# Reading the moving operand of the feed-forward products in turn from the two halves of its row

## The chip, the cores and the metric

The kernel runs on one core of one Trainium2 chip. The metric is the time of one execution on the device, in microseconds. Before the change it is 862.88 us, the median of three runs (862.77 to 863.19).

## The reference

A retention layer (attention without softmax, with a decay that falls with the distance of the positions) is followed by two feed-forward layers. The batch is 4, with 8 heads, 576 positions and a head dimension of 64, so that 2304 tokens of width 512 reach the feed-forward layers. Everything is float32.

```
scores = (q @ k.T) / sqrt(64)                # for each batch and head
ret    = scores * D                          # D[i,j] = gamma_h**(i-j) for j <= i, else 0
x      = ret @ v                             # -> 2304 x 512
x      = lrelu(x @ moe_w_in) @ moe_w_out     # 512 -> 2048 -> 512, slope 0.01
y      = elu(x @ moe2_w_in) @ moe2_w_out     # 512 -> 2048 -> 512, alpha 1
```

## The kernel before, in words

The tokens stand in five blocks (`SIZES`): four of 512 (128 positions of each of the four batch entries) and a small one of 256. The 2048 hidden features are cut into 16 groups of 128, and those into four quarters of four groups (`NQ`, `FQ`). A unit of work is (layer `m`, quarter `q`, block, group); the units run in that order, so that for each quarter all five blocks are passed.

Each float32 product is made from three products in the float32r type. Every operand is split into a rounded part and a rest (`wh`, `wl` for weights, `xh`, `xl` for the input, `gh`, `gl` for the activated hidden values), and high times high, low times high and high times low are summed in one bank of PSUM.

`moe_h` makes the hidden values of a unit: 12 products (L399), with a 128 x 128 piece of the input weights as the stationary operand and 512 tokens as the moving operand. The result is 128 features by 512 tokens. ScalarE and VectorE apply the nonlinearity and split the result into `gh` and `gl`. `moe_y`, three units later (`LAG`), makes the second product of a unit, 12 products again (L538). In the first layer the output weights are stationary and the 512 tokens of `gh` or `gl` move, so that the result is features by tokens, which is what the next layer reads. In the second layer a 128 x 128 piece of `gh` or `gl` is stationary and the 512 columns of the output weights `wh` or `wl` move, so that the result is tokens by features, as the output is stored. `evac` adds each quarter's result to a sum in SBUF; at the last quarter the first layer's sum is split into the next layer's `xh` and `xl`, and the second layer's is stored.

The block of 256 tokens goes through `moe_h_small` and `moe_y_small`. There the high and the low part lie side by side in one tile of 512 columns, so that one product covers both (L426, L478), and a second product of 256 columns (L431, L478) adds the low part of the weights. In the second layer L478 moves 512 columns of the output weights, as L538 does; the last tile of the kernel is made in two cuts of 256 columns.

In all cases the moving operand is read as one run of 4-byte columns that follow each other in SBUF, and the result is written as one run in PSUM.

The program writes the order of the work out by hand. The retention steps (20 of them) are set between the first units; their products are small float32 ones (L204, L239, L250, L262, L297). Before them TensorE runs 18 products of 512 bfloat16 columns on idle data (L628) in two groups of nine, each with the same stationary operand. The weights come in by the SP queue in pieces of 512 KB and are unpacked and split by ScalarE and VectorE (`split_a`, `split_b`, `split_c`). In `split_a` ScalarE reads every second 4-byte word of the loaded tile (L345, L347):

```
two = raws.pop(key).rearrange("p (n t) -> p n t", t=2)
low, high = two[:, :, 0], two[:, :, 1]
```

Of the kernel before, what the change touches and what calls it, by code (L numbers as in the profile page):

```python
# [17 lines left out]
NT, DM, DFF = B * S, H * D, 2048  # L18
# [11 lines left out]
BOUNDS = [sum(SIZES[:i]) for i in range(len(SIZES) + 1)]  # L30
# [15 lines left out]
def _turned(x):  # L46

    x = x.copy()
    x[:, ::2] = np.roll(x[:, ::2], HC, axis=0)
    return x  # L50


def _decays():
# [30 lines left out]
def retention_moe(  # L84
# [15 lines left out]
    nc = tc.nc  # L100
# [12 lines left out]
    def bank(tag, bufs):  # L113
        return psum.tile([P, 512], F32, tag=tag, bufs=bufs, name=f"ps_{tag}")
# [58 lines left out]
    xx = xpool.tile([P, KC, 2 * SMALL], F32R, tag="xx", name="xx")  # L173
# [206 lines left out]
    gs = {}  # L380
    yb = {}

    def moe_h(u):
        m, q, blk, fs = u
        n = SIZES[blk]
        if blk == NMAIN:
            return moe_h_small(u)
        h = bank("h", 4)
        for i, f in enumerate(fs):
            wh, wl = weights["i", (m * NQ + q) * FQ + f]  # L390
            ops = []
            for kk in range(KC):
                w = slice(kk * P, (kk + 1) * P)
                ops += [(wh[:, w], xh[blk][:, kk, :]), (wl[:, w], xh[blk][:, kk, :])]
            for kk in range(KC):
                w = slice(kk * P, (kk + 1) * P)
                ops += [(wh[:, w], xl[blk][:, kk, :])]
            for k, (a, x) in enumerate(ops):
                nc.tensor.matmul(  # L399
                    h[:, i * n : (i + 1) * n], a, x, start=k == 0, stop=k == len(ops) - 1  # L400
                )
        g = gpool.tile([P, NMAX], F32, tag="g", name="g")
        gh = gpool.tile([P, NMAX], F32R, tag="gh", name="gh", bufs=LAG + 1)
        gl = gpool.tile([P, NMAX], F32R, tag="gl", name="gl", bufs=LAG + 1)
        if m == 0:
            nc.scalar.activation(gh, h, AF.Prelu, alpha=0.01)  # L406
            nc.scalar.activation(g, h, AF.Prelu, alpha=0.01)  # L407
        else:
            nc.scalar.activation(g, h, AF.Relu, scale=-1.0)  # L409
            nc.scalar.activation(g, g, AF.Exp, scale=-1.0)  # L410
            nc.vector.scalar_tensor_tensor(g, g, -1.0, h, ALU.add, ALU.max)  # L411
            nc.vector.tensor_copy(gh, g)
        nc.vector.tensor_tensor(gl, g, gh.bitcast(F32), ALU.subtract)  # L413
        gs[u] = gh, gl

    def moe_h_small(u):

        m, q, blk, fs = u
        n = SMALL
        hs = gpool.tile([P, NMAX], F32, tag="g", name="hs")  # L420
        for i, f in enumerate(fs):
            wh, wl = weights["i", (m * NQ + q) * FQ + f]
            h = bank("h", 4)
            for kk in range(KC):
                w = slice(kk * P, (kk + 1) * P)
                nc.tensor.matmul(  # L426
                    h, wh[:, w], xx[:, kk, :], start=kk == 0, stop=False, skip_group_check=True
                )
            for kk in range(KC):
                w = slice(kk * P, (kk + 1) * P)  # L430
                nc.tensor.matmul(  # L431
                    h[:, :n], wl[:, w], xh[blk][:, kk, :],
                    start=False, stop=kk == KC - 1, skip_group_check=True,
                )
            t = hs[:, i * n : (i + 1) * n]
            nc.scalar.activation(t, h[:, n:], AF.Copy)
            nc.vector.tensor_tensor(t, t, h[:, :n], ALU.add)
        if m == 0:
            g = hs
            nc.scalar.activation(g, hs, AF.Prelu, alpha=0.01)  # L440
        else:
            g = gpool.tile([P, NMAX], F32, tag="g", name="g")
            nc.scalar.activation(g, hs, AF.Relu, scale=-1.0)
            nc.scalar.activation(g, g, AF.Exp, scale=-1.0)
            nc.vector.scalar_tensor_tensor(g, g, -1.0, hs, ALU.add, ALU.max)
        both = []
        for i, tag in enumerate(("gh", "gl")):
            t = gpool.tile([P, NMAX], F32R, tag=tag, name=tag, bufs=LAG + 1)
            part = g[:, i * n : (i + 1) * n]
            nc.scalar.activation(t[:, :n], part, AF.Copy)  # L450
            nc.vector.tensor_tensor(t[:, n:], part, t.bitcast(F32)[:, :n], ALU.subtract)
            both.append(t)
        gs[u] = both

    def moe_y_small(u):
        m, q, blk, fs = u
        n = SMALL
        both = gs.pop(u)
        parts = KC if m == 0 else n // P
        if fs[0] == 0:  # L460
            yb[blk] = [bank("y", 4) for _ in range(parts)]
        y = yb[blk]

        last = m == 1 and q == NQ - 1 and fs[-1] == FQ - 1
        for e in range(parts):
            cuts = [slice(0, DM // 2), slice(DM // 2, DM)] if last and e == parts - 1 else [slice(0, DM)]
            for cut in cuts:
                for t, f in zip(both, fs):
                    wh, wl = weights["o", (m * NQ + q) * FQ + f]
                    if m == 0:  # L470
                        w = slice(e * P, (e + 1) * P)
                        ops = (y[e], wh[:, w], t), (y[e][:, :n], wl[:, w], t[:, :n])
                    else:
                        a, b = t[:, e * P : (e + 1) * P], t[:, n + e * P : n + (e + 1) * P]
                        o = y[e][:, cut]
                        ops = (o, a, wh[:, cut]), (o, a, wl[:, cut]), (o, b, wh[:, cut])
                    for k, (o, a, x) in enumerate(ops):
                        nc.tensor.matmul(  # L478
                            o, a, x, start=f == 0 and k == 0,
                            stop=f == FQ - 1 and k == len(ops) - 1, skip_group_check=True,  # L480
                        )
        if fs[-1] == FQ - 1:
            evac_small(m, q, blk, yb.pop(blk))
# [33 lines left out]
    def moe_y(u):  # L517

        m, q, blk, fs = u
        if blk == NMAIN:  # L520
            return moe_y_small(u)
        gh, gl = gs.pop(u)
        n = SIZES[blk]
        parts, cols = (KC, n) if m == 0 else (n // P, DM)
        if fs[0] == 0:
            yb[blk] = [bank("y", 4)[:, :cols] for _ in range(parts)]
        y = yb[blk]
        for e in range(parts):
            for i, f in enumerate(fs):
                wh, wl = weights["o", (m * NQ + q) * FQ + f]  # L530
                if m == 0:
                    w, g = slice(e * P, (e + 1) * P), slice(i * n, (i + 1) * n)
                    ops = (wh[:, w], gh[:, g]), (wh[:, w], gl[:, g]), (wl[:, w], gh[:, g])
                else:
                    g = slice(i * n + e * P, i * n + (e + 1) * P)
                    ops = (gh[:, g], wh), (gh[:, g], wl), (gl[:, g], wh)
                for k, (a, x) in enumerate(ops):
                    nc.tensor.matmul(  # L538
                        y[e], a, x, start=f == 0 and k == 0, stop=f == FQ - 1 and k == 2
                    )  # L540
        if fs[-1] == FQ - 1:
            evac(m, q, blk, cols, yb.pop(blk))

    def evac(m, q, blk, cols, y):
        if q == 0:
            yp[blk] = big.tile([P, 4, 512], F32, tag="big", name="yp")
        a = yp[blk]
        for e in range(len(y)):
            t = a[:, e, :cols]
            if q == 0:  # L550
                nc.scalar.activation(t, y[e], AF.Copy)
            else:
                nc.vector.tensor_tensor(t, t, y[e], ALU.add)  # L553
            if q == NQ - 1 and m == 0:
                nc.scalar.activation(xh[blk][:, e, :cols], t, AF.Copy)
                nc.gpsimd.tensor_tensor(
                    xl[blk][:, e, :cols], t, xh[blk].bitcast(F32)[:, e, :cols], ALU.subtract
                )
            if q == NQ - 1 and m == 1:
                t0 = BOUNDS[blk] + e * P  # L560
                nc.sync.dma_start(out=out[t0 : t0 + P, :], in_=t)
# [35 lines left out]
    with tc.manual_schedule():  # L597
        qk, v, k = slice(0, 2), slice(2, 3), slice(3, 4)
# [69 lines left out]
        for n in range(len(units) + LAG):  # L668
            u = units[n] if n < len(units) else None
            p = units[n - LAG] if n >= LAG else None  # L670
            s = nxt if nxt < nsteps else None
# [10 lines left out]
            if u:  # L682
                moe_h(u)
# [25 lines left out]
            if p:  # L709
                moe_y(p)  # L710
# [61 lines left out]
```

## Time and profile before

| | |
|---|---|
| median of three runs | 862.88 us (862.77 to 863.19) |
| span of the profiled execution | 862.2 us; it stands 0.7 us under the median |
| TensorE (PE), matmuls | 850.8 us busy, 99% of the span |
| VectorE (DVE) | 502.5 us, 58% |
| ScalarE (ACT) | 347.8 us, 40% |
| GpSimd (POOL) | 85.4 us, 10% |
| mean granted TensorE clock | 0.999 of full speed |

The profile shows one execution. The times of the three runs stand without a profile of their own, so the profiled execution is known by its span, from the first to the last instruction. Matmuls overlap in the records, since each one's recorded length reaches past the start of the next; the rate of TensorE is read from the distance between starts, not from the recorded lengths.

### The profile page before, as it was taken

How to read it: one execution, taken by the hardware profiler on the slowest of the kernel's cores; microseconds unless marked ns; L12 is line 12 of the kernel's file. 1: busy time of each engine (PE TensorE's matmuls, PEld its weight loads, DVE VectorE, ACT ScalarE, POOL GpSimd, SP SyncE). 2: the span in 40 equal slices, each digit the busy share in tenths (PEclk: the TensorE clock that was granted, in tenths of full speed). 3: DMA queues.
4: the chain of work that ended last, by engine and by line, in shares of the span. 5: the costliest groups of instructions: out<-in, count | busy, mean ns of one | idle time of the engine just before them, and what ended most of it. 6: DMA issues, size and time to landing. Idle time of an engine off the chain costs nothing.

```text
span 862.2 us, 11733 instructions
## 1 busy us (share of the span) xinstructions
PE 850.8 (99%) x4664; PEld 702.8 (82%) x4664; DVE 502.5 (58%) x889; ACT 347.8 (40%) x631; POOL 85.4 (10%) x88
## 2 busy tenths in 40 slices
PE   8899999999999999999999999999999999999998
PEld 5778887888888888888888888888888888888886
DVE  5998952465254652556345873657656784675443
ACT  3455444543233432345344643554234442532222
POOL 2564421000000000002222100000000000000000
PEclk9999999999999999999999999999999999999999
DMA  9984420121000220112000220102101220001112
GB/s 335 329 303 145 157 79 9 49 98 50 1 29 21 74 74 1 49 49 69 30 25 25 74 74 0 50 31 68 49 10 40 74 74 0 25 1 49 49 50 74
DMA packets 23143, 60.15 MB, mean 70 GB/s; under 512 B 2864, under 2 KB 6192, under 8 KB 23088
## 3 DMA queue, kind: packets, MB, share of 16 engines
q1 hardware_dynamic: 22800, 59.26, 20.2%
q8 instruction: 37, 0.61, 0.3%
q10 hardware_dynamic: 288, 0.14, 0.1%
q14 instruction: 18, 0.15, 0.1%
HBM read 54.66 MB, written 4.72 MB: 69 GB/s over the span
## 4 chain that ended last, share of the span: by engine, by line
PE 95%; DVE 2%; DMA 1%; ACT 0%; POOL 0%; issue 0%; SPq 0%; DVEq 0%; POOLq 0%
PE ps_y L538 41%; PE ps_h L399 40%; PE ps_y L478 5%; PE ps_h L426 3%; PE ps_h L431 2%; PE ps_h L204 1%; PE ps_h L250 1%; DMA ain<-in_att 1%; DVE ain L222 0%; PE ps_h L297 0%; PE ps_h L262 0%; PE ps_h L239 0%; DVE pf L226 0%; PE ps_y L204 0%; DVE u L362 0%
## 5 line engine op out<-in xcount | busy, mean ns | idle before, releaser
L399 PE MATMUL ps_h<-xh,wil 128*128 128x512 f32 x512 | 199.6, 390 | 1.9 <-POOL wil L375 1.9
L399 PE MATMUL ps_h<-xh,wih 128*128 128x512 f32 x512 | 199.9, 390 | 0.9 <-ACT wih L373 0.6
L413 DVE TENSOR_TENSOR gl<-g,gh 128x512 fp32r<-128x512 f32 x128 | 91.0, 711 | 174.1 <-ACT g L407 168.5
L399 PE MATMUL ps_h<-xl,wih 128*128 128x512 f32 x512 | 136.9, 389 | 0.0
L406 ACT ACTIVATE gh<-ps_h 128x512 fp32r<-128x512 f32 x64 | 38.2, 597 | 196.5 <-PE ps_h L399 196.4
L411 DVE SCALAR_TENSOR_TENSOR g<-g,ps_h 128x512 f32<-128x512 f32 x64 | 44.0, 687 | 122.1 <-ACT g L410 121.9
L399 PEld LDWEIGHTS ps_h<-xh,wil 128*128 128x128 f32 x512 | 96.1, 188 | 22.2 <-POOL wil L375 2.5
L399 PEld LDWEIGHTS ps_h<-xh,wih 128*128 128x128 f32 x512 | 96.1, 188 | 21.5 <-ACT wih L373 1.0
L399 PEld LDWEIGHTS ps_h<-xl,wih 128*128 128x128 f32 x512 | 96.1, 188 | 20.2
L409 ACT ACTIVATE g<-ps_h 128x512 f32<-128x512 f32 x64 | 38.2, 597 | 180.0 <-PE ps_h L399 180.0
L538 PE MATMUL ps_y<-gh,woh 128*128 128x512 f32 x256 | 101.3, 396 | 0.0
L538 PE MATMUL ps_y<-gh,wol 128*128 128x512 f32 x256 | 100.1, 391 | 0.7 <-POOL wol L375 0.7
L538 PE MATMUL ps_y<-gl,woh 128*128 128x512 f32 x256 | 99.8, 390 | 0.0
L538 PE MATMUL ps_y<-woh,gl 128*128 128x512 f32 x256 | 99.7, 390 | 0.0
L538 PE MATMUL ps_y<-wol,gh 128*128 128x512 f32 x256 | 99.7, 390 | 0.0
L538 PE MATMUL ps_y<-woh,gh 128*128 128x512 f32 x256 | 99.6, 389 | 0.0
L553 DVE TENSOR_TENSOR yp<-yp,ps_y 128x512 f32<-128x512 f32 x96 | 59.4, 680 | 0.0
L538 PEld LDWEIGHTS ps_y<-gh,wol 128*128 128x128 f32 x256 | 48.0, 188 | 11.5 <-POOL wol L375 1.1
L538 PEld LDWEIGHTS ps_y<-gh,woh 128*128 128x128 f32 x256 | 48.0, 188 | 10.7 <-ACT woh L373 0.2
L538 PEld LDWEIGHTS ps_y<-woh,gl 128*128 128x128 f32 x256 | 48.1, 188 | 10.1
L538 PEld LDWEIGHTS ps_y<-wol,gh 128*128 128x128 f32 x256 | 48.0, 188 | 9.8
L538 PEld LDWEIGHTS ps_y<-woh,gh 128*128 128x128 f32 x256 | 48.0, 188 | 9.7
(106 smaller groups left out, 1104.6 us busy)
## 6 DMA issues: line engine op xcount, KB each, us to landing
raw<-in_moe_in SPq DMA_DIRECT2D x32, 512.0 KB, 3.3
raw<-in_moe_out SPq DMA_DIRECT2D x32, 512.0 KB, 3.3
ain<-in_att SPq DMA_DIRECT2D x16, 512.0 KB, 6.8
ain<-in_att SPq DMA_DIRECT2D x20, 256.0 KB, 7.3
out<-yp SPq DMA_DIRECT2D x17, 256.0 KB, 2.2
kn<-in_att SPq DMA_DIRECT2D x12, 256.0 KB, 6.2
st<-in_near_v SPq DMA_DIRECT2D x32, 64.0 KB, 5.4
ain<-in_tail_qk SPq DMA_DIRECT2D x4, 256.0 KB, 3.2
```

What stands on the lines that cost most here:

```text
L204: nc.tensor.matmul(sc[j][keys[j], pr * n : (pr + 1) * n], t[r, 1, pr * n : (pr + 1) * n], t[r, 0, pr * n : (pr + 1) * n], start=True, stop ...
L250: nc.tensor.matmul(x[half[j], pr * n : (pr + 1) * n], st[b][:, j, pr, :], t[:, 2 * j, pr * n : (pr + 1) * n], start=pr == 0, stop=n < CH, ...
L399: nc.tensor.matmul(h[:, i * n : (i + 1) * n], a, x, start=k == 0, stop=k == len(ops) - 1)
L406: nc.scalar.activation(gh, h, AF.Prelu, alpha=0.01)
L409: nc.scalar.activation(g, h, AF.Relu, scale=-1.0)
L411: nc.vector.scalar_tensor_tensor(g, g, -1.0, h, ALU.add, ALU.max)
L413: nc.vector.tensor_tensor(gl, g, gh.bitcast(F32), ALU.subtract)
L426: nc.tensor.matmul(h, wh[:, w], xx[:, kk, :], start=kk == 0, stop=False, skip_group_check=True)
L431: nc.tensor.matmul(h[:, :n], wl[:, w], xh[blk][:, kk, :], start=False, stop=kk == KC - 1, skip_group_check=True,)
L478: nc.tensor.matmul(o, a, x, start=f == 0 and k == 0, stop=f == FQ - 1 and k == len(ops) - 1, skip_group_check=True,)
L538: nc.tensor.matmul(y[e], a, x, start=f == 0 and k == 0, stop=f == FQ - 1 and k == 2)
L553: nc.vector.tensor_tensor(t, t, y[e], ALU.add)
```

## The change

A new helper `product` issues every product of both feed-forward layers. It hands TensorE the moving operand in another order: column 0, then the first column of the second half, then column 1, then the second column of the second half, and so on. For 512 columns the two halves are 256 columns, 1024 bytes, apart. Where a tile holds a high and a low part side by side (`parts` is 2), each part has its own two halves, and for an operand of 256 columns the halves are 128 columns, 512 bytes, apart. The result is still written as one run in PSUM, so that each such product leaves its columns in a shuffled order: the tokens of a block are shuffled once more by each of the first three products, and the host puts them right at the end (`_in_order`). In the last product the weights move, and the host shuffles the columns of `moe2_w_out` beforehand so that the features come out in order. The number of instructions, the data that each reads, the stationary operands, the retention part and the transfers' sizes are unchanged.

```diff
+def _in_order(y):
+    for _ in range(3):
+        y = y.reshape(-1, 2, DM).transpose(1, 0, 2).reshape(-1, DM)
+    return y
...
+    def product(out, w, x, parts=1, cut=None, **flags):
+        if parts == 1:
+            x = x.rearrange("p (a n) -> p n a", a=2)
+            if cut:
+                x = x[:, cut.start // 2 : cut.stop // 2, :]
+            out = out.rearrange("p (n a) -> p n a", a=2)
+        else:
+            x = x.rearrange("p (s a n) -> p s n a", s=parts, a=2)
+            out = out.rearrange("p (s n a) -> p s n a", s=parts, a=2)
+        nc.tensor.matmul(out, w, x, **flags)
...
     def moe_h(u):
...
-                nc.tensor.matmul(
-                    h[:, i * n : (i + 1) * n], a, x, start=k == 0, stop=k == len(ops) - 1
-                )
+                product(h[:, i * n : (i + 1) * n], a, x, start=k == 0, stop=k == len(ops) - 1)
...
     def moe_h_small(u):
...
-                nc.tensor.matmul(
-                    h, wh[:, w], xx[:, kk, :], start=kk == 0, stop=False, skip_group_check=True
+                product(
+                    h, wh[:, w], xx[:, kk, :], 2, start=kk == 0, stop=False, skip_group_check=True
                 )
...
-                nc.tensor.matmul(
+                product(
                     h[:, :n], wl[:, w], xh[blk][:, kk, :],
...
     def moe_y_small(u):
...
-                        ops = (y[e], wh[:, w], t), (y[e][:, :n], wl[:, w], t[:, :n])
+                        ops = (y[e], wh[:, w], t, 2), (y[e][:, :n], wl[:, w], t[:, :n])
                     else:
                         a, b = t[:, e * P : (e + 1) * P], t[:, n + e * P : n + (e + 1) * P]
                         o = y[e][:, cut]
-                        ops = (o, a, wh[:, cut]), (o, a, wl[:, cut]), (o, b, wh[:, cut])
-                    for k, (o, a, x) in enumerate(ops):
-                        nc.tensor.matmul(
-                            o, a, x, start=f == 0 and k == 0,
+                        ops = (o, a, wh, 1, cut), (o, a, wl, 1, cut), (o, b, wh, 1, cut)
+                    for k, op in enumerate(ops):
+                        product(
+                            *op, start=f == 0 and k == 0,
...
     def moe_y(u):
...
-                    nc.tensor.matmul(
+                    product(
                         y[e], a, x, start=f == 0 and k == 0, stop=f == FQ - 1 and k == 2
...
-        arrays[f"{m}_out"] = np.ascontiguousarray(inputs[f"{m}_w_out"]).view(np.int64)
+        w = np.asarray(inputs[f"{m}_w_out"])
+        if m == "moe2":
+            w = w.reshape(DFF, DM // 2, 2).transpose(0, 2, 1).reshape(DFF, DM)
+        arrays[f"{m}_out"] = np.ascontiguousarray(w).view(np.int64)
...
     y = r.results[0]["out_0"]
+    y = np.concatenate([_in_order(y[a:b]) for a, b in zip(BOUNDS, BOUNDS[1:])])
```

## Rows read from the trace of the kernel before

**Rows 1.** The page: engines' busy time (share, instructions), and the granted clock.

```profile
PE 850.8 (99%) x4664; PEld 702.8 (82%) x4664; DVE 502.5 (58%) x889; ACT 347.8 (40%) x631; POOL 85.4 (10%) x88
...
PEclk9999999999999999999999999999999999999999
```

**Rows 2.** The page: the chain that ended last, by line.

```profile
PE ps_y L538 41%; PE ps_h L399 40%; PE ps_y L478 5%; PE ps_h L426 3%; PE ps_h L431 2%; PE ps_h L204 1%; PE ps_h L250 1%; DMA ain<-in_att 1%; DVE ain L222 0%; PE ps_h L297 0%; PE ps_h L262 0%; PE ps_h L239 0%; DVE pf L226 0%; PE ps_y L204 0%; DVE u L362 0%
```

**Rows 3.** Groups by line and shape: xcount, busy us, mean recorded ns, idle.

```profile
L399 PE MATMUL ps_h<-xh,wih 128*128 128x512 f32 x512 | 199.9, 390 | 0.9 <-ACT wih L373 0.6 <-ACT xh L275 0.2
...
L538 PE MATMUL ps_y<-gh,woh 128*128 128x512 f32 x256 | 101.3, 396 | 0.0
...
L426 PE MATMUL ps_h<-xx,wih 128*128 128x512 f32 x128 | 34.7, 393 | 0.0
...
L431 PE MATMUL ps_h<-xx,wil 128*128 128x256 f32 x128 | 20.3, 280 | 0.0
...
L478 PE MATMUL ps_y<-gh,woh 128*128 128x512 f32 x32 | 12.7, 396 | 0.0
...
L478 PE MATMUL ps_y<-gh,wol 128*128 128x256 f32 x32 | 9.0, 280 | 0.0
```

**Rows 4.** TensorE in order of time, 299 to 304 us: start, length.

```profile
299.64 0.39 PE L399 MATMUL ps_h<-xh,wih 128*128 128x512 f32 x1
...
300.55 1.07 PE L399 MATMUL ps_h<-xl,wih 128*128 128x512 f32 x4
...
303.95 0.39 PE L538 MATMUL ps_y<-gh,wol 128*128 128x512 f32 x1
```

**Rows 5.** TensorE in order of time at the start: the bfloat16 products.

```profile
1.19 3.53 PE L628 MATMUL ps_h<-pf 128*128 128x512 bf16 x8 [1.19 <-DVE pf L622]
...
6.22 2.12 PE L628 MATMUL ps_h<-pf 128*128 128x512 bf16 x9
```

**Rows 6.** Line 628 by itself: recorded ns, min/median/max.

```profile
L628 PE MATMUL ps_h<-pf x18: 379/385/634, 1.2 to 8.0; 128*128 128x512 bf16 x18
```

**Rows 7.** TensorE in order of time, 268.5 to 270.3 us: widths alternate.

```profile
268.51 0.39 PE L478 MATMUL ps_y<-gh,woh 128*128 128x512 f32 x1
268.74 0.28 PE L478 MATMUL ps_y<-gh,wol 128*128 128x256 f32 x1
268.85 0.40 PE L478 MATMUL ps_y<-gl,woh 128*128 128x512 f32 x1
...
270.26 0.40 PE L478 MATMUL ps_y<-gl,woh 128*128 128x512 f32 x1
```

**Rows 8.** TensorE in order of time, 250 us: four products of 256 columns.

```profile
250.16 0.64 PE L431 MATMUL ps_h<-xx,wil 128*128 128x256 f32 x4
250.63 0.40 PE L426 MATMUL ps_h<-xx,wih 128*128 128x512 f32 x1
```

**Rows 9.** Groups by line: ScalarE reads with and without a step.

```profile
L345 ACT ACTIVATE u<-raw 128x512 f32<-128x512 f32 x64 | 42.8, 669 | 21.5 <-DVE wol L375 15.5 <-DMA raw<-in_moe_in 5.3 <-DMA raw<-in_moe_out 0.6
...
L410 ACT ACTIVATE g<-g 128x512 f32<-128x512 f32 x64 | 40.4, 632 | 2.0
```

**Rows 10.** Stretches: length, busy us of PE, PEld, DVE, ACT, POOL.

```profile
20.00:40.00 20.00, 17.81 (x228) 14.35 (x226) 18.71 (x38) 9.06 (x16) 9.87 (x10) 1.00 1.04 324
40.00:60.00 20.00, 18.34 (x229) 15.04 (x228) 17.84 (x31) 12.09 (x21) 12.13 (x13) 1.00 1.01 340
60.00:100.00 40.00, 40.00 (x377) 33.28 (x375) 34.71 (x58) 19.76 (x35) 21.53 (x24) 1.00 0.48 166
...
600.00:700.00 100.00, 100.00 (x450) 83.03 (x449) 67.21 (x121) 39.04 (x69) 0.00 (x0) 1.00 0.14 47
```

**Rows 11.** Lines 399 and 538 alone, first 60 us: busy PE, PEld.

```profile
0.00:60.00 60.00, 15.52 (x60) 10.95 (x60) 1.00 0.98 334
...
0.00:60.00 60.00, 3.27 (x12) 2.10 (x12) 1.00 0.98 334
```

**Rows 12.** Weight loads (PEld) by line: xcount, busy us, mean recorded ns.

```profile
L399 PEld LDWEIGHTS ps_h<-xh,wih 128*128 128x128 f32 x512 | 96.1, 188 | 21.5 <-ACT wih L373 1.0 <-ACT xh L275 0.4
```

## The prediction

> **What bounds the kernel now.** I read the page first. TensorE's matmuls are busy for 850.8 of 862.2 us and the granted clock is full in all forty slices [rows 1]; the chain that ended last lies almost wholly on TensorE, 81% of it on L538 and L399 alone and most of the rest on L478, L426 and L431 [rows 2]. So the kernel is one long queue of matmuls, and what changes the distance between two of them changes the time in full. The recorded lengths (390 ns for 512 columns [rows 3]) overlap and don't give that distance, so next I read TensorE in order of time: from 299.64 to 303.95 us there are 19 steps between starts, through both lines and both layers' kinds of operand [rows 4], hence 4.31 / 19 = 226.8 ns a product.
>
> [...] The bfloat16 products at the start have the same 512 columns and a weight load before each; nine of them end 2.12 us after the first began [rows 5], and as one alone is recorded with 379 ns [rows 6], eight steps take 1.74 us: 217.5 ns each. [...]
>
> **The change part by part.** Nothing is added or removed as an instruction, and the result in PSUM stays one run, so the evacuations by ScalarE and VectorE are as before. The host's shuffles are outside the measured time; the weights of the second layer come in the same 512 KB pieces. The retention products keep their order. All that changes is the order in which a product fetches its columns, and so the term is (number of products) x (change of one).
>
> The number, from the groups [rows 3] and the code's loops: L399 3 x 512 = 1536; L538 6 x 256 = 1536; L426 128; L478 64 in the first layer and 90 in the second. That is 3354 of 512 columns. Of 256 columns there are 128 (L431), 64 and 12 (L478), together 204.
>
> The change of one. No row shows TensorE reading in such an order, so I bound it from both sides. [...] By the bfloat16 row it falls to 217.5, which saves 9.3 ns; that row fits what the new order does, for each half of the row is then read at half the rate, 4 bytes every second cycle, as many bytes per cycle as a bfloat16 operand takes from its one run. I take 11 ns, between these two: the eight bfloat16 steps include the first one after a pause, so 217.5 is a little high. Above: the nearest operation with a step is ScalarE's, which reads every second word in 669 ns where it reads adjacent words in 632 [rows 9], 6% more; on 226.8 ns that is +13.3 ns. That is far from TensorE, and I use it as the upper bound of the milder loss only.
>
> The sum: 3354 x 11 ns = 36.9 us. For the 204 of 256 columns I take half, 5 ns: 1.0 us. From this goes what lies in the first 60 us, where VectorE is busy for 18.7 and 17.8 of 20 us [rows 10] and sets the pace: 60 products of L399 and 12 of L538 [rows 11], 72 x 11 ns = 0.8 us. The gain is 37 us. Against the profiled execution that is 862.2 - 37 = 825.2 us, and with the 0.7 us by which it stands under the median, about 826 us. The likeliest case's own range follows from 9.3 and 13.5 ns: 3354 x 9.3 = 31 us and 3354 x 13.5 + 204 x 6.7 = 47 us, so 816 to 832 us.
>
> What covers the rest when TensorE is faster: after the first 100 us VectorE is busy for at most 67.2 of 100 us, ScalarE less [rows 10]; with 5% less time that is 71%, no bound. From 60 to 100 us VectorE has 34.7 of 40 us [rows 10], 91% after a gain of 5%: near, but not the bound. The weight loads are recorded with 188 ns each [rows 12], below 216, and begin when the matmul before begins, so they should stay hidden behind 512 columns; behind 256 they may be the limit already, which is why I take only 5 ns there.
>
> **The rivals.**
> [...]
>
> A milder loss. Switching between the halves costs something, but a few per cent: up to +13.3 ns by ScalarE's row, 3354 x 13.3 = 45 us, up to 908 us. Nothing else speaks for a size between this and half the speed.
>
> [...]
>
> [...]
>
> **How the numbers follow.** I give the full gain 0.49, the part 0.11, no change 0.14, the milder loss 0.07 and half the speed 0.19. A difference of 0.2% (1.7 us) is about what a measurement of this kernel can tell from none. So faster is 0.60, same 0.14, slower 0.26. The predicted time is 826 us. The range begins at 815, just under the largest gain, and must reach over the part, no change and the milder loss, to 908 us and rounded to 910; left out are half the speed at 0.19 and little else.
>
> **What the profile after would show.** If I am right, the distance between starts of 512-column products is 214 to 218 ns, in L399 and L538 alike, the recorded length falls from 390 towards 379 ns, and TensorE stays the chain. [...] The prediction would be wrong also if the gain shows in one line and not in the other, since the operands lie in different tiles, or if in the first 100 us waits on VectorE take the place of the shorter products.

## The result and the profile after

The changed kernel takes 824.09 us (median of four runs, 823.24 to 824.92) against 863.04 us of the kernel before, run beside it. The ratio is 0.9546, with a 95% interval of 0.9533 to 0.956: 38.95 us, or 4.5%, less.

The page of the kernel after: busy time by engine, and the granted clock.

```profile
PE 810.3 (99%) x4664; PEld 705.7 (86%) x4664; DVE 514.8 (63%) x889; ACT 373.0 (45%) x631; POOL 88.1 (11%) x88
...
PEclk9999999999999999999999999999999999999999
```

Against [rows 1], TensorE's matmuls are busy for 40.5 us less in as many instructions, still 99% of the span; the mean granted clock is 1.000 of full speed, where it was 0.999. VectorE and ScalarE are busy for 12 and 25 us more with the same number of instructions; this comes back below.

The chain that ended last, by line. All products of the feed-forward layers now stand under the helper's line, L401.

```profile
PE ps_y L401 45%; PE ps_h L401 45%; DMA ain<-in_att 2%; PE ps_h L211 1%; PE ps_h L257 1%; DMA ot_sb<-in_otab 1%; DVE ain L229 0%; PE ps_h L304 0%; PE ps_h L269 0%; DVE pf L233 0%; DVE xt L288 0%; DVE u L369 0%; SPq L154 0%; DVE u L371 0%; POOL wol L382 0%
```

Nothing has taken TensorE's place: 90% of the chain lies on the same products that held 91% before [rows 2].

TensorE of the kernel after in order of time, as in [rows 4] and [rows 7]: start, recorded length.

```profile
299.75 0.38 PE L401 MATMUL ps_y<-gh,woh 128*128 128x512 f32 x1
...
303.85 0.38 PE L401 MATMUL ps_h<-xh,wil 128*128 128x512 f32 x1
...
240.92 0.61 PE L401 MATMUL ps_h<-xx,wil 128*128 128x256 f32 x4
241.37 1.03 PE L401 MATMUL ps_h<-xx,wih 128*128 128x512 f32 x4
...
258.25 0.38 PE L401 MATMUL ps_y<-gh,woh 128*128 128x512 f32 x1
258.47 0.27 PE L401 MATMUL ps_y<-gh,wol 128*128 128x256 f32 x1
...
260.21 0.38 PE L401 MATMUL ps_y<-gh,woh 128*128 128x512 f32 x1
```

From 299.75 to 303.85 us there are 19 steps through the second product of one unit and the first of another: 215.8 ns each, where it was 226.8. Four products of 256 columns take 0.45 us, not 0.47 [rows 8]. Where widths of 512 and 256 alternate, six pairs take 1.96 us, 327 ns a pair, not 350.

### The profile page after: what moved, and what is told of

It is laid out like the page before. It is cut to its first block, busy times and chain, and to the rows that moved or that the text cites. A ratio compares the mean times of both kernels' runs of the same rounds, so it can differ in the third digit from the quotient of the medians.

```text
span 822.1 us, 11715 instructions
## 1 busy us (share of the span) xinstructions
PE 810.3 (99%) x4664; PEld 705.7 (86%) x4664; DVE 514.8 (63%) x889; ACT 373.0 (45%) x631; POOL 88.1 (11%) x88
## 4 chain that ended last, share of the span: by engine, by line
PE 94%; DMA 2%; DVE 2%; ACT 0%; POOL 0%; issue 0%; SPq 0%; DVEq 0%; POOLq 0%
PE ps_y L401 45%; PE ps_h L401 45%; DMA ain<-in_att 2%; PE ps_h L211 1%; PE ps_h L257 1%; DMA ot_sb<-in_otab 1%; DVE ain L229 0%; PE ps_h L304 0%; PE ps_h L269 0%; DVE pf L233 0%; DVE xt L288 0%; DVE u L369 0%; SPq L154 0%; DVE u L371 0%; POOL wol L382 0%
## 5 line engine op out<-in xcount | busy, mean ns | idle before, releaser
L401 PE MATMUL ps_h<-xh,wil 128*128 128x512 f32 x512 | 194.3, 379 | 1.9 <-POOL wil L382 1.9
L401 PE MATMUL ps_h<-xh,wih 128*128 128x512 f32 x512 | 194.5, 380 | 1.3 <-ACT wih L380 1.1
L401 PE MATMUL ps_h<-xl,wih 128*128 128x512 f32 x512 | 131.4, 379 | 0.0
L401 PE MATMUL ps_y<-gh,woh 128*128 128x512 f32 x288 | 110.6, 384 | 0.3 <-ACT woh L380 0.3
L401 PEld LDWEIGHTS ps_h<-xh,wil 128*128 128x128 f32 x512 | 96.8, 189 | 15.9 <-POOL wil L382 2.5
L401 PEld LDWEIGHTS ps_h<-xh,wih 128*128 128x128 f32 x512 | 96.8, 189 | 15.5 <-ACT wih L380 1.4
L401 PE MATMUL ps_y<-woh,gh 128*128 128x512 f32 x290 | 109.4, 378 | 0.0
L401 PE MATMUL ps_y<-woh,gl 128*128 128x512 f32 x290 | 109.4, 378 | 0.0
L401 PE MATMUL ps_y<-gl,woh 128*128 128x512 f32 x288 | 109.2, 379 | 0.0
L401 PEld LDWEIGHTS ps_h<-xl,wih 128*128 128x128 f32 x512 | 96.8, 189 | 13.7
L401 PE MATMUL ps_y<-gh,wol 128*128 128x512 f32 (+1 forms) x288 | 105.8, 368 | 0.7 <-POOL wol L382 0.7
L401 PE MATMUL ps_y<-wol,gh 128*128 128x512 f32 x273 | 103.3, 378 | 0.0
L352 ACT ACTIVATE u<-raw 128x512 f32<-128x512 f32 x64 | 56.2, 878 | 20.5 <-DVE wol L382 15.1
L401 PEld LDWEIGHTS ps_y<-gh,woh 128*128 128x128 f32 x288 | 54.4, 189 | 8.8 <-ACT woh L380 0.5
L401 PEld LDWEIGHTS ps_y<-gh,wol 128*128 128x128 f32 x288 | 54.5, 189 | 8.2 <-POOL wol L382 1.1
L401 PEld LDWEIGHTS ps_y<-woh,gl 128*128 128x128 f32 x290 | 54.8, 189 | 7.7
L401 PEld LDWEIGHTS ps_y<-woh,gh 128*128 128x128 f32 x290 | 54.8, 189 | 7.6
L401 PEld LDWEIGHTS ps_y<-gl,woh 128*128 128x128 f32 x288 | 54.5, 189 | 7.2
```

The costliest lines, as they stand in the source:

```text
L352: nc.scalar.activation(u, high.bitcast(F32), AF.Abs, scale=2.0**16)
L401: nc.tensor.matmul(out, w, x, **flags)
```

## The experiments

All twelve kernels keep the schedule. Ten change the order of the columns in the large blocks' products, 3072 of 512 columns; unless said otherwise the block of 256 tokens keeps the halves of the change (the second layer's weights take the new order there too), and the host undoes each order. For these ten the edits below show only the new order of `x`, the moving operand, not the helper code around it. Distances are read from starts around 300 us, as in [rows 4]. Where no range stands beside a time, the kernel was run once.

Three things in the expectations are assumptions of mine and no readings: how long a cycle is, on which the 267 ns for the step of four and the 427 ns for the quarters rest; the 13.5 ns of the first expectation, since the shortest distance that any run shows for these products is 215 ns, 12 less than in the old order; and that a moving operand is fetched in lines or stretches that have to be opened.

**What the 11 ns belong to.** Two kernels start from the old order.

```diff
+                c = P if k % 2 == 0 and k < 2 * KC else P // 2
                 nc.tensor.matmul(
-                    h[:, i * n : (i + 1) * n], a, x, start=k == 0, stop=k == len(ops) - 1
+                    h[:c, i * n : (i + 1) * n], a[:, :c], x,
+                    start=k == 0, stop=k == len(ops) - 1, skip_group_check=True,
```

> The order of the columns is the old one. In the large blocks' first product (the 1536 of 512 columns in moe_h) the eight of twelve that bring a low part load only 64 of the 128 stationary columns; the low parts of the other 64 features are left out. If the extra 13.5 ns belong to the stream of the moving operand, the distance between starts stays at 227 ns and the time at 863 us. If they belong to the weight load, the eight lose half of them: 6.7 ns x 1024 = 7 us, about 856 us, with distances of 220 ns where half-size loads follow each other.

It took 867.41 us (four runs, 867.2 to 867.48); ratio 1.0046 (1.0029 to 1.0063). TensorE in order of time:

```profile
299.82 0.39 PE L400 MATMUL ps_h<-xh,wih 128*128 128x512 f32 x1
300.05 0.40 PE L400 MATMUL ps_h<-xh,wil 128*64 128x512 f32 x1
...
300.74 1.08 PE L400 MATMUL ps_h<-xl,wih 128*64 128x512 f32 x4
301.65 0.39 PE L540 MATMUL ps_y<-gh,woh 128*128 128x512 f32 x1
```

Four products in a row with half of the stationary columns take 0.91 us, 227.5 ns each; where wide and narrow alternate, four steps take 0.92 us, 230 ns. The weight loads did get shorter in the records:

```profile
L400 PEld LDWEIGHTS ps_h<-xl,wih 128*64 128x64 f32 x512 | 68.5, 134 | 47.8
```

134 ns against 188 [rows 12], and the distance didn't fall. It doesn't follow the length of the weight load. (That the steps are 2.5 ns longer where the width alternates was not expected and wasn't pursued.)

```diff
-                    h[:, i * n : (i + 1) * n], a, x, start=k == 0, stop=k == len(ops) - 1
+                    h[:, i * n : (i + 1) * n], a, x[:, 0:1].to_broadcast([P, n]),
+                    start=k == 0, stop=k == len(ops) - 1
...
-                        y[e], a, x, start=f == 0 and k == 0, stop=f == FQ - 1 and k == 2
+                        y[e], a, x[:, 0:1].to_broadcast([P, x.shape[-1]]),
+                        start=f == 0 and k == 0, stop=f == FQ - 1 and k == 2
```

> In the 3072 products of the large blocks the moving operand is its first column, repeated 512 times; the result is that of one token (or one output feature), the other columns' work is left out. If a cycle is lost each time the in-order read opens a new stretch of memory, nothing is opened and the distance falls to about 216 ns: 863 - 3072 x 11 ns = 829 us. If 4-byte columns can't be taken at more than 16 in 17 cycles, whatever the address, or if the weight load is the cause, it stays at 227 ns and 863 us.

It took 831.3 us.

```profile
299.62 0.38 PE L399 MATMUL ps_h<-xh,wil 128*128 128x512 f32 x1
...
302.87 0.38 PE L539 MATMUL ps_y<-gh,wol 128*128 128x512 f32 x1
...
L399 PEld LDWEIGHTS ps_h<-xh,wih 128*128 128x128 f32 x512 | 97.9, 191 | 15.2 <-ACT wih L373 0.9
```

15 steps in 3.25 us are 216.7 ns each, 10.1 less than the 226.8 of the old order. As many 4-byte columns enter each product, and the weight loads are no shorter (191 ns, 188 before [rows 12]). So these 10 ns belong to fetching new columns in order; the weight load doesn't set them, and since the halves bring as many new columns at 215.8 ns, neither does the number of bytes.

**How far apart the two stretches must be.**

```diff
-            x = x.rearrange("p (a n) -> p n a", a=2)
+            x = x.rearrange("p (b a n) -> p b n a", a=2, n=4)     # near4
+            x = x.rearrange("p (b a n) -> p b n a", a=2, n=16)    # near16
```

> In turn from two stretches of 16 bytes side by side: columns 0, 4, 1, 5, 2, 6, 3, 7, then 8, 12, and so on, in the large blocks' products. If the reader holds the lines that it has opened, so that each is fetched once for four columns, this is as good as the halves: 216 ns, 826 us. If it fetches anew at each column, and the halves are fast because they lie in different parts of the memory, two neighbouring lines may lie in one part: then up to the 460 ns of the step of four, 1590 us.

> In turn from two stretches of 64 bytes side by side: columns 0, 16, 1, 17, up to 15, 31, then 32, 48, and so on. If half the rate per stretch is what hides the opening, the distance of the two doesn't matter: 216 ns, 826 us. If each new 64 bytes costs its cycle as in the old order, 227 ns and 863 us. If the halves' far distance puts them into different parts of the memory and this one doesn't, up to 460 ns and 1590 us.

They took 823.96 and 823.65 us. Eight steps of the one, then eight of the other:

```profile
299.68 0.38 PE L431 MATMUL ps_y<-gh,woh 128*128 128x512 f32 x1
...
301.40 0.38 PE L431 MATMUL ps_y<-gh,wol 128*128 128x512 f32 x1
```

```profile
299.79 0.38 PE L431 MATMUL ps_y<-gh,wol 128*128 128x512 f32 x1
...
301.52 0.38 PE L431 MATMUL ps_y<-gl,woh 128*128 128x512 f32 x1
```

215 and 216 ns, beside the halves' 215.8. Two stretches of 16 or of 64 bytes side by side are as good as two halves 1024 bytes apart; between these three the distance of the stretches doesn't matter.

**Longer runs from each half.**

```diff
-            x = x.rearrange("p (a n) -> p n a", a=2)
+            x = x.rearrange("p (a n r) -> p n a r", a=2, r=16)    # run16
+            x = x.rearrange("p (a n r) -> p n a r", a=2, r=4)     # run4
+            x = x.rearrange("p (a n r) -> p n a r", a=2, r=2)     # run2
```

> The moving operand is read in runs of 16 columns (64 bytes) from the two halves in turn: columns 0 to 15, 256 to 271, 16 to 31, and so on. If the gain comes from reading each half at half the rate, so that a stretch can be opened while the other half supplies a column, runs of 16 give nothing: 227 ns, 863 us. If it is enough that neighbouring stretches aren't opened one after the other, it is 216 ns and 826 us.

> Runs of four columns (16 bytes) from the two halves in turn: 0 to 3, 256 to 259, 4 to 7, and so on. [...] If only crossing 64 bytes within one stream costs a cycle, each half crosses as often as in the old order: 227 ns, 863 us, or 216 ns if the other half's turn hides it.

> Runs of two columns from the halves in turn: 0, 1, 256, 257, 2, 3, and so on. [...] If alternating hides the opening as soon as no stream runs longer than the 8 bytes of a pair, 216 ns and 826 us.

They took 899.23, 929.83 and 1190.93 us. TensorE of each in order of time, 13, 11 and 3 steps:

```profile
299.67 0.40 PE L431 MATMUL ps_y<-gh,wol 128*128 128x512 f32 x1
...
302.79 0.40 PE L431 MATMUL ps_h<-xh,wih 128*128 128x512 f32 x1
```

```profile
299.69 0.41 PE L431 MATMUL ps_h<-xl,wih 128*128 128x512 f32 x1
...
302.44 0.42 PE L431 MATMUL ps_y<-gl,woh 128*128 128x512 f32 x1
```

```profile
300.72 0.50 PE L431 MATMUL ps_y<-gh,woh 128*128 128x512 f32 x1
...
301.72 0.50 PE L431 MATMUL ps_y<-gh,woh 128*128 128x512 f32 x1
```

240, 250 and 333 ns: all slower than the 226.8 of the old order, and none at the 216 or 227 ns expected. Runs of 2, 4 and 16 columns from each half are a loss; a single column from each is the gain.

**One stream with a step, and two of them.**

```diff
-            x = x.rearrange("p (a n) -> p n a", a=2)
+            x = x.rearrange("p (n a) -> p a n", a=2)              # step2
+            x = x.rearrange("p (n a) -> p a n", a=4)              # step4
+            x = x.rearrange("p (a n k) -> p k n a", a=2, k=4)     # two_step4
+            x = x.rearrange("p (a n) -> p n a", a=4)              # quarters
```

> One stream with a step of two columns (0, 2, 4, ..., then 1, 3, 5, ...): two uses of each 16 bytes. [...] If the loss is one per 16 columns whatever their distance, 227 ns and 863 us.

> The moving operand of the large blocks' products is read with a step of four columns (0, 4, 8, ..., then 1, 5, 9, ...), one stream with one use of each 16 bytes at a time; the host puts the order right. If a cycle is lost with every new 64 bytes, four columns share a loss: 128 cycles per 512 columns, 267 ns, and 863 + 3072 x 40 ns = 986 us. [...] If the loss belongs only to reads of neighbouring columns, it is 216 ns and 829 us.

> In turn from the two halves, but each half with a step of four columns: 0, 256, 4, 260, 8, 264, ..., then 1, 257, 5, 261, and so on, so that each column lies in a 16-byte line that neither of the three before it touched, and no line is used again soon. [...] If the reader holds the lines that it has opened and the halves are fast because each line serves more columns, nothing is held here: 460 ns and 1590 us.

> In turn from the four quarters: 0, 128, 256, 384, 1, 129, and so on. If several streams share the opening, four are as good as two: 216 ns, 826 us. If the fast form is bound to two (two ports, or two lines held), each column opens anew: 427 to 460 ns, 1480 to 1590 us.

They took 1567.61, 1592.97, 1567.42 and 1033.22 us. TensorE of each in order of time, 6, 7, 4 and 4 steps:

```profile
299.52 0.63 PE L431 MATMUL ps_h<-xh,wil 128*128 128x512 f32 x1
...
302.22 0.63 PE L431 MATMUL ps_h<-xh,wil 128*128 128x512 f32 x1
```

```profile
299.76 0.64 PE L431 MATMUL ps_y<-gh,woh 128*128 128x512 f32 x1
...
302.98 0.64 PE L431 MATMUL ps_h<-xh,wil 128*128 128x512 f32 x1
```

```profile
299.77 0.63 PE L431 MATMUL ps_h<-xh,wih 128*128 128x512 f32 x1
...
301.58 0.63 PE L431 MATMUL ps_h<-xh,wih 128*128 128x512 f32 x1
```

```profile
300.80 0.45 PE L431 MATMUL ps_y<-gh,woh 128*128 128x512 f32 x1
...
301.93 0.45 PE L431 MATMUL ps_y<-gl,woh 128*128 128x512 f32 x1
```

450, 460, 452 and 282 ns. For the steps of two and of four and for the quarters none of the figures worked out before came true. The step of four in two alternating halves is only 8 ns faster than alone. So alternating by itself gains next to nothing: of the orders here that alternate single columns of two stretches, only those gained whose columns in each stretch are neighbours. And four streams of neighbours are no gain at all: 282 ns is 55 more than the old order takes.

**Whether a version is faster still.**

```diff
-            x = x.rearrange("p (a n) -> p n a", a=2)
+            x = x.rearrange("p (b a n) -> p b n a", a=2, n=16)
...
-            x = x.rearrange("p (s a n) -> p s n a", s=parts, a=2)
+            x = x.rearrange("p (b a n) -> p b n a", a=2, n=16)
```

> As the run with stretches of 64 bytes side by side (0, 16, 1, 17, ...), now also in the block of 256 tokens. In the changed kernel ScalarE's reads with a step rose from 669 to 878 ns and VectorE's from 739 to 924; with neighbouring stretches they were 695 and 758. If these longer reads hold up the first 60 us, where VectorE is busy for 19.0 of 20 us, this version gains some tenths of a us: 823.5 us. If TensorE alone sets the time, it is as fast as the change: 824 us, ratio 0.954 to 0.955.

It took 823.62 us (five runs, 823.52 to 824.25); ratio 0.9544 (0.953 to 0.9557). Beside the change's 0.9546 (0.9533 to 0.956) that is no difference. The two expectations, 823.5 and 824 us, lie too close together for these runs to choose between them: whether the longer reads cost some tenths of a us is not shown.

## Why the prediction was right

- **The bound, and that nothing takes its place.** Right. The time fell by what TensorE's products lost, and the chain stays on them. VectorE, at 68.9 of 100 us in the stretch that had 67.2 [rows 10], sets nothing there.
- **The change of one product.** Forecast 11 ns, measured 226.8 - 215.8 = 11.0. That is 1.7 ns under the 217.5 read from the bfloat16 products, which the prediction called a little high. No run shows the 13.5 and 6.7 ns that the range's lower end is worked out with: products of 512 columns gained 11.0 ns, those of 256 columns 7.
- **The 256 columns.** Forecast 5 ns; 0.47 to 0.45 us for four is 5 ns each, but the starts are shown to 0.01 us only. Over the whole traces such a step falls from 118.0 to 110.9 ns, 7 ns, so this term was a little small. The alternating pairs gained 23 ns, not 16.
- **The sum.** 3354 x 11.0 = 36.9, 128 x 5 = 0.6 and 64 x (23 - 11) = 0.8 us make 38.3 us. The spans differ by 862.2 - 822.1 = 40.1 us, the medians by 38.95 us. The two traces, with their 4664 matmuls matched one by one, show where the 1.8 us between sum and spans lie. Of the lead, 0.7 us stand before 24 us and come mostly from earlier transfers (next point). After the first 60 us the gain is 39.2 us: 36.2 us on 3173 steps from one product of 512 columns to the next, 11.4 ns each (11 in most, 14 to 24 in some that follow soon after narrower products); 1.5 us on 97 steps from 512 to 256 columns, 15.6 ns each; and 1.4 us on 203 steps from a product of 256 columns, 7.1 ns each.
- **The deduction for the first 60 us** held, though it looks wrong at first. The chain's piece of twelve L538 products that begins at 60.12 us before begins at 59.34 after, as if all of 72 x 11 ns had been kept although VectorE is busy for 18 to 19 of 20 us there. But most of this lead was there before a product of the feed-forward layers had run: 0.56 us at 12 us, where the kernel before waits longer for a transfer. At 24 us, after the first twelve of these products, it is 0.71 us. From there to the piece at 60.12 us lie 60 products, worth 60 x 11 = 660 ns, and the lead grew by 0.07 us only. The kernel with halved weight loads, in which these products gained nothing, begins the same piece at 59.29 us.

TensorE's first matmul after that transfer, the first VectorE piece of the chain after 24 us, and the piece near 60 us, of the kernel before and of the kernel after; then that last piece of the kernel with halved weight loads:

```profile
12.33 1.16 PE L204 MATMUL ps_y<-ain 64*128 64x128 f32 x16 [0.34 <-DMA ain<-in_att]
...
24.08 0.69 DVE ain L222
...
60.12 2.97 PE ps_y L538 x12
```

```profile
11.77 1.16 PE L211 MATMUL ps_y<-ain 64*128 64x128 f32 x16
...
23.37 0.68 DVE ain L229
...
59.34 2.79 PE ps_y L401 x12
```

```profile
59.29 2.95 PE ps_y L540 x12
```

- **The reason given for 11 ns was only partly right.** That they belong to fetching the moving operand is shown by the repeated column, which gains 10.1 of them (216.7 ns), and by the halved weight loads, which gain none (227.5 ns). That each half gains because it is read at half the rate, every second column, is not enough: two halves with a step of four are read at that rate too and take 452 ns. The bfloat16 row gave the right size without giving the mechanism, and that 11 ns were met to the tenth is luck: the working gave a reason for more than 9.3 ns, and none for 11.
- **The rivals.** No change, whether from the weight load or from a limit in bytes, fell with the same two runs and the 215.8 ns of the halves, and a part of the gain with the 11.0 ns. Losses of the milder size exist, though for another order than the change: runs of 16 cost the 13 ns that I had priced for it. Half the speed is real and near: orders one short step away take 450 to 460 ns, about twice the 226.8 of the old order; what makes them slow, the runs don't show. How often an order uses the same 16 bytes in a row, counted column by column, doesn't sort them: the step of two has two uses of each 16 bytes in a row and takes 450 ns, the halves have one at a time and take 216.

What count would sort them all? One that takes every second column of an order. Then the halves, both near orders and the repeated column have four or more uses in a row of the same 16 bytes (0, 1, 2, 3): 215 to 217 ns. The old order and the runs of 16 and of 4 have two (0, 2, then 4, 6): 227 to 250. Runs of two, the quarters and all steps have one: 282 to 460. This was formed after the last run and fits all of them; no run was chosen to test it, it names no cause, and it doesn't explain the spread within a group. It remains a supposition.

## What to carry to other kernels

Read the distance between starts of matmuls and compare it with that of other products of as many columns in the same trace, as here with the 217.5 ns of the bfloat16 ones: 5% (11.0 of 226.8 ns) lay in the order of the columns alone, unseen in the busy share, which was 99% before and after. With 4-byte moving operands like these (float32r), alternate single columns of two runs of neighbours: 215.8 ns with runs of 1024 bytes here, and still 215 with runs of 16 bytes. Measure the very order before building on it, since orders that look alike (quarters, pairs, a step of two) made a product 24%, 47% and 98% longer than the old order.

## What the runs showed of the hardware that was not expected

With the halves, other engines' reads with a step became slower although they do the same work. ScalarE's and VectorE's reads of every second word of the loaded weights (busy, mean ns): VectorE's of the kernel before, whose ScalarE row is in [rows 9], then both of the kernel after, then of the kernel with stretches of 64 bytes side by side:

```profile
L362 DVE SCALAR_TENSOR_TENSOR u<-u,raw 128x512 uint32<-128x512 uint32 x64 | 47.3, 739 | 2.2
```

```profile
L369 DVE SCALAR_TENSOR_TENSOR u<-u,raw 128x512 uint32<-128x512 uint32 x64 | 59.1, 924 | 2.2
L352 ACT ACTIVATE u<-raw 128x512 f32<-128x512 f32 x64 | 56.2, 878 | 20.5 <-DVE wol L382 15.1 <-DMA raw<-in_moe_in 5.3
...
L428 ACT ACTIVATE g<-g 128x512 f32<-128x512 f32 x64 | 40.4, 632 | 2.1
```

```profile
L389 DVE SCALAR_TENSOR_TENSOR u<-u,raw 128x512 uint32<-128x512 uint32 x64 | 48.5, 758 | 2.2
L372 ACT ACTIVATE u<-raw 128x512 f32<-128x512 f32 x64 | 44.5, 695 | 20.4 <-DVE wol L402 15.0 <-DMA raw<-in_moe_in 5.3
```

ScalarE's went from 669 [rows 9] to 878 ns and VectorE's from 739 to 924, while ScalarE's read of adjacent words stayed at 632. With neighbouring stretches they are 695 and 758, at the same speed of TensorE, and 677 and 734 once the block of 256 tokens has them too. Runs of four from the halves show it too:

```profile
L372 ACT ACTIVATE u<-raw 128x512 f32<-128x512 f32 x64 | 55.1, 862 | 21.6 <-DVE wol L402 16.0 <-DMA raw<-in_moe_in 5.4
```

Runs of 16 and of two from the same halves don't (690 and 696 ns), so the distance of the halves isn't the whole cause, and I leave it open. It cost no time that the runs can tell (823.62 us without it, 824.09 with it), since neither engine sets the pace for most of the span. In a kernel bound by them it may, which no run here shows; the near order all but avoids it.
